# GEGLU on one core: eight first products ahead of the second ones, and another order of the first loads

## The chip, the cores and the metric

The kernel runs on one core of one Trainium2 chip. The metric is the device time of one execution in microseconds (us).

## The reference

```python
B, S, D, F = 32, 32, 1024, 3584        # x [32, 32, 1024], all bf16
def reference(x, w_gate, w_up, w_down):
    return (gelu_tanh(x @ w_gate) * (x @ w_up)) @ w_down
```

The 1024 rows of x are tokens. The output is [32, 32, 1024] in bf16.

## The kernel before

Both stages are block products of 2 x 2 halves done with seven multiplications instead of eight (sums and differences of the halves take the place of one product).

**Stage 1.** The left operand has w_gate and w_up as its two rows and the two halves of D as its columns: A11 and A12 are the low and the high half of D of w_gate, A21 and A22 those of w_up. The right operand is x transposed: B11 and B21 are the low and the high half of D for tokens 0 to 511, B12 and B22 the same for tokens 512 to 1023. F is cut into 28 blocks of 128 columns. For a block `i`:

- the first product A11 B11 and the second A12 B21 add up in one PSUM bank to w_gate's result for the first tokens. Each is four matmuls of 128x128 by 128x512 in bf16. Between them ScalarE copies the first product out to `E1` (an eviction), and after the second it applies GELU from the bank into `GL`;
- the five others (`fourth_product` to `seventh_products`, `third_product`) use sums in float32r: S1 to S4 of weights, T1 to T4 of x. A seed (`seed`) copies `E1` back into a bank, on which the sixth, seventh and fourth products go on.

First and second products run ahead of the rest by ten blocks (`LEAD`). The order of instructions on each engine is the order of the code (`tc.manual_schedule`), so each engine's queue is a list written by hand.

**Loads.** `load_gate(c, queue, lo, hi)` loads 256 columns of w_gate (blocks 2c and 2c + 1) and of them the slices lo to hi of the eight 128-row slices of D. Slices 0 to 3 (`0, KH`) are called the low half of gate c here, 4 to 7 (`KH, DT`) the high half; each is 256 KB. Gates 0 to 3 have buffers of their own, gates 4 and 5 lie in a part of `gT` that is written late. `load_up(c, lo, hi)` loads w_up. x comes by three transposing DMAs on SP's queue: B11 (L131), B21 (L147) and both halves for the later tokens, `xt1` (L154). DMAs are issued from two queues, SP (`nc.sync`) and ScalarE (`nc.scalar`). [...]

**Start.** While B11 is on its way TensorE runs ten warm-up matmuls on constants (L139) into four PSUM banks `warm`. After warm-up matmuls 3 and 7 ScalarE makes a small copy from the bank (L141), which delays the loads that stand behind it in ScalarE's queue.

**PSUM.** Eight banks in two rings of four: `psum_q` (tag "q") for first and second products and later `Y`, `psum_p` (tag "p") for the warm-up and then `X`.

**Order of TensorE before.** First products of blocks 0 and 1 (in two cuts of D), 2, 3; second products of 0 to 3; then for 4, 6 and 8 the first products of a pair, one operation on ScalarE (`between`), and its second products. After that come `Y` of blocks 0 and 1 with T1 (timeline: y<-T,s), first products of block 10, the sixth products with T2 (x<-T,s), and so on. VectorE makes S1 to S4 of blocks 0 and 1 from w_up's first load, then T1 to T4 (L165) when `xt1` has landed.

**Stage 2** is the same scheme with w_down and `gT`; the change does not touch it.

Of the kernel before, what the change touches and what calls it, by code (L numbers as in the profile page):

```python
# [7 lines left out]
ACT = mybir.ActivationFunctionType  # L8
# [4 lines left out]
def kernel(  # L13
# [18 lines left out]
    nc = tc.nc  # L32
# [10 lines left out]
    DT = D // P  # L43
    KH = DT // 2
# [31 lines left out]
    B11, B21 = xt0[:, :KH, :], xt0[:, KH:, :]  # L76
# [6 lines left out]
    def load_gate(c, queue, lo=0, hi=DT):  # L83
        if c not in WG:
            WG[c] = gw.tile([P, DT, 2 * P], bf16, name="gw", tag="gw")
        queue.dma_start(  # L86
            out=WG[c][:, lo:hi, :], in_=wg_r[:, lo:hi, 2 * c * P : (2 * c + 2) * P]
        )

    def load_up(c, lo=0, hi=4):  # L90
        if c not in WU:
            WU[c] = uw.tile([P, DT, 4 * P], bf16, name="uw", tag="uw")
        nc.sync.dma_start(
            out=WU[c][:, :, lo * P : hi * P],
            in_=wu_r[:, :, (4 * c + lo) * P : (4 * c + hi) * P],
        )
# [4 lines left out]
    def a11(i):  # L101
        return block(WG, 2, i, 0)

    def a12(i):
        return block(WG, 2, i, 1)
# [4 lines left out]
    def a22(i):  # L110
        return block(WU, 4, i, 1)
# [12 lines left out]
    def psum_p(name):  # L124
        return psum.tile([P, NB], fp32, name=name, tag="p")

    def psum_q(name):
        return psum.tile([P, NB], fp32, name=name, tag="q")

    with tc.manual_schedule():  # L130
# [4 lines left out]
        table = opool.tile([P, 8], bf16, name="table", tag="o")  # L135
        nc.scalar.activation(table, ones[:, 0:8], ACT.Gelu_apprx_tanh)  # L136

        for n in range(NWARM):
            nc.tensor.matmul(warm[n % 4], lhsT=ones[:, 0:P], rhs=ones, start=True, stop=True)  # L139
            if n in (3, 7):  # L140
                nc.scalar.activation(table, warm[n % 4][:, 0:8], ACT.Copy)  # L141
            if n == 3:
                load_gate(0, nc.scalar, 2, KH)
                load_gate(1, nc.scalar, 0, KH)
            if n == 7:
                load_gate(0, nc.scalar, KH, DT)
        nc.sync.dma_start_transpose(out=B21, in_=xf[0:NB, KH * P : D])  # L147
        load_gate(1, nc.sync, KH, DT)
        load_gate(2, nc.sync)
        load_gate(3, nc.sync, 0, KH)  # L150
        load_up(0, 0, 2)
        load_gate(3, nc.sync, KH, DT)
        load_gate(4, nc.sync)
# [8 lines left out]
        def t_sum(name, a, b, step=2):  # L162
            for k in range(0, KH, step):
                ks = slice(k, k + step)
                nc.vector.tensor_tensor(T[name][:, ks, :], a[:, ks, :], b[:, ks, :], ALU.subtract)  # L165
# [19 lines left out]
        def copy_a22(i):  # L185
            nc.scalar.activation(C22[i], a22(i), ACT.Copy)

        A, E1, GL = {}, {}, {}

        def pair_product(ps, lhs, rhs, first, cuts):  # L190
            for lo, hi in zip(cuts, cuts[1:]):
                for p, l in zip(ps, lhs):
                    for k in range(lo, hi):
                        nc.tensor.matmul(  # L194
                            p,
                            lhsT=l[:, k, :],
                            rhs=rhs[:, k, :],
                            start=(first and k == 0),
                            stop=(k == KH - 1),
                            skip_group_check=True,  # L200
                        )

        def first_products(*blocks, cuts=(0, KH)):
            for i in blocks:
                A[i] = psum_q("a")
            pair_product([A[i] for i in blocks], [a11(i) for i in blocks], B11, True, cuts)
            for i in blocks:
                if i % 2 == 0:
                    pool, tag = (xpool, "e1") if i == LEAD - 2 else (ring, "ring")
                    E1[i // 2] = pool.tile([P, 2, NB], fp32, name="e1", tag=tag)  # L210
                nc.scalar.activation(E1[i // 2][:, i % 2, :], A[i], ACT.Copy)  # L211

        def second_products(*blocks, cuts=(0, KH)):
            pair_product([A[i] for i in blocks], [a12(i) for i in blocks], B21, False, cuts)
            for i in blocks:
                if i % 2 == 0:
                    GL[i // 2] = half.tile([P, 2, NB], bf16, name="gl0", tag="half")
                nc.scalar.activation(GL[i // 2][:, i % 2, :], A[i], ACT.Gelu_apprx_tanh)
# [3 lines left out]
        def seed(i):  # L222
            X[i] = psum_p("x")
            nc.scalar.activation(X[i], E1[i // 2][:, i % 2, :], ACT.Copy)
# [3 lines left out]
        def ahead():  # L228
            nonlocal done
            if done < FT:  # L230
                first_products(done)
            second_products(done - 1)
            done += 1
# [40 lines left out]
        t_sum("T2", B22, T["T1"])  # L274
        t_sum("T3", B22, B12)
        t_sum("T4", B21, T["T2"])
        between = {4: lambda: seed(0), 6: lambda: seed(1), 8: lambda: copy_a22(0)}
        first_products(0, 1, cuts=(0, 2, KH))
        first_products(2)
        first_products(3)  # L280
        for n in range(4):
            second_products(n)
        for n in (4, 6, 8):
            first_products(n)
            first_products(n + 1)
            between[n]()
            second_products(n)
            second_products(n + 1)
        for k in range(KH):
            nc.scalar.activation(T["B22"][:, k, :], B22[:, k, :], ACT.Copy)  # L290
        copy_a22(1)
# [25 lines left out]
        for i in range(2, FT + 1):  # L317
# [24 lines left out]
            if here and i % 2 == 0:  # L342
                c = i // 2 + (6 if i < 8 else 4)
# [44 lines left out]
        B21 = lambda j: V21[j]  # L388
# [149 lines left out]
```

## Time and profile before

| | |
|---|---|
| time, median of 3 runs | 276.35 us (276.2 to 276.45) |
| profiled execution | 276.38 us, of which the span in the trace 274.6 us |
| TensorE clock granted | 1.00 over the whole span |
| last copy out of PSUM starts, last store issued | 271.25 us, 271.87 us |

Times in the views are counted from the start of the span. PE is TensorE, DVE VectorE, ACT ScalarE, POOL GpSimd, SP the engine that only issues; SPq and ACTq are the issues of DMAs on SP's and ScalarE's queue, and the length of such a row is how long the issue held the engine, not the transfer. In a timeline the columns are start, length, engine, line, operation, output <- inputs, shapes, number, and in brackets the idle time before the group and what ended it. In a row of a DMA queue stand packets, MB and the time that the packets took as a share of 16 engines. In a row of a DMA issue stand number, KB each and us from the start of the issue to the landing.

### The profile page before, as it was taken

To read this page: it belongs to the slowest core of one execution; us is meant where nothing else is said; L and a number is where in the kernel's file an instruction comes from. 1 tells how busy PE (TensorE), PEld (TensorE's weight loads), DVE (VectorE), ACT (ScalarE), POOL (GpSimd) and SP (SyncE) were. 2 spreads that over 40 slices of the span, in tenths; PEclk is the share of its full clock that TensorE was granted. 3 is DMA by queue.
4 is the path that set the end of the run, shared out by engine and by line. 5 is a ranking of instruction groups with operands and counts; after the bars stand their busy time and mean duration, and the time that the engine had idled before them with its cause. 6 is when DMAs were issued, how large, how long until landed. Compare 5 with 4: busy or idle time off the path is not lost.

```text
span 274.6 us, 3345 instructions
## 1 busy us (share of the span) xinstructions
PE 269.2 (98%) x1186; PEld 189.6 (69%) x1186; DVE 188.7 (69%) x226; ACT 138.1 (50%) x238; POOL 87.1 (32%) x81
## 2 busy tenths in 40 slices
PE   8899999999999999999999999999999999999995
PEld 2345667768777687776877768764447888888883
DVE  0078875866667666686666766769994999999900
ACT  2588665666556665566665666531100072860311
POOL 0000083845558455584455844600000000000000
PEclk9999999999999999999999999999999999999999
DMA  8999402153400034216260202359702000000321
GB/s 173 295 289 236 155 1 76 35 197 91 140 2 0 0 90 143 76 28 203 87 220 0 76 2 76 107 195 319 223 0 76 2 0 0 1 2 0 116 76 38
DMA packets 40992, 26.42 MB, mean 96 GB/s; under 512 B 9232, under 2 KB 40976, under 8 KB 40976
## 3 DMA queue, kind: packets, MB, share of 16 engines
q1 hardware_dynamic: 39232, 25.30, 31.9%
q10 hardware_dynamic: 1744, 0.92, 1.2%
q8 instruction: 9, 0.15, 0.2%
q14 instruction: 7, 0.06, 0.1%
HBM read 22.02 MB, written 2.10 MB: 88 GB/s over the span
## 4 chain that ended last, share of the span: by engine, by line
PE 96%; DMA 2%; ACT 1%; ACTq 0%; issue 0%
PE x L194 19%; PE x L393 18%; PE y L115 18%; PE a L194 17%; PE x L115 9%; PE y L393 9%; PE z L393 4%; DMA gw<-in_w_gate_dram 2%; PE y L194 1%; ACT L136 0%; ACTq L86 0%; ACT o_sb L505 0%; ACT table L136 0%; ACT table L141 0%
## 5 line engine op out<-in xcount | busy, mean ns | idle before, releaser
L194 PE MATMUL x<-T,s 128*128 128x512 f32 x224 | 63.5, 407 | 0.0
L194 PEld LDWEIGHTS x<-T,s 128*128 128x128 f32 x224 | 41.7, 188 | 10.7
L194 PE MATMUL a<-xt,gw 128*128 128x512 bf16 x192 | 44.8, 380 | 1.3 <-DMA gw<-in_w_gate_dram 0.8
L257 DVE TENSOR_TENSOR u<-y,e 128x512 bf16<-128x512 f32 x28 | 19.3, 691 | 33.2 <-ACT e L255 32.4
L183 POOL TENSOR_TENSOR s<-gw,s 128x512 fp32r<-128x512 bf16 x22 | 26.0, 1181 | 48.5 <-PE y L115 47.8
L194 PEld LDWEIGHTS <-gw 128*128 128x128 bf16 x192 | 17.3, 98 | 25.3 <-issue 5.7
L179 DVE TENSOR_TENSOR s<-s,gw 128x512 fp32r<-128x512 f32 x24 | 34.5, 1436 | 0.0
L264 ACT ACTIVATE gl<-h 128x512 bf16<-128x512 bf16 x28 | 17.7, 631 | 28.1 <-DVE h L262 28.1
L244 DVE TENSOR_TENSOR gT<-gl,x 128x512 bf16<-128x512 bf16 x28 | 19.2, 687 | 17.6 <-PE x L115 17.6
L115 PE MATMUL x<-T,c 128*128 128x512 f32 x112 | 30.3, 393 | 0.0
L115 PE MATMUL y<-B,s 128*128 128x512 f32 x112 | 30.2, 391 | 0.0
L174 POOL TENSOR_TENSOR s<-uw 128x512 fp32r<-128x512 bf16 x25 | 29.1, 1165 | 0.0
L115 PE MATMUL y<-T,s 128*128 128x512 f32 x104 | 27.8, 389 | 0.0
L211 ACT ACTIVATE e<-a 128x512 f32<-128x512 f32 x28 | 16.6, 597 | 18.7 <-PE a L194 18.6
L393 PE MATMUL x<-tc,sc 128*128 128x512 f32 x112 | 25.7, 389 | 0.0
L255 ACT ACTIVATE e<-x 128x512 f32<-128x512 f32 x28 | 16.7, 600 | 16.0 <-PE x L194 16.0
L175 POOL TENSOR_TENSOR s<-gw,uw 128x512 fp32r<-128x512 bf16 x21 | 24.4, 1162 | 0.0
L115 PEld LDWEIGHTS y<-B,s 128*128 128x128 f32 x112 | 21.0, 188 | 4.8
L115 PEld LDWEIGHTS x<-T,c 128*128 128x128 f32 x112 | 20.9, 188 | 4.8 <-ACT e L255 0.5
L393 PEld LDWEIGHTS x<-tc,sc 128*128 128x128 f32 x112 | 21.0, 188 | 4.4
L115 PEld LDWEIGHTS y<-T,s 128*128 128x128 f32 x104 | 19.5, 188 | 4.1
L393 PEld LDWEIGHTS <-gT 128*128 128x128 bf16 x112 | 10.9, 98 | 13.3 <-issue 0.3
(56 smaller groups left out, 347.0 us busy)
## 6 DMA issues: line engine op xcount, KB each, us to landing
uw<-in_w_up_dram SPq DMA_DIRECT2D x6, 1024.0 KB, 6.5
gw<-in_w_gate_dram SPq DMA_DIRECT2D x9, 512.0 KB, 4.0
v<-in_w_down_dram SPq DMA_DIRECT2D x5, 512.0 KB, 3.9
v<-in_w_down_dram SPq DMA_DIRECT2D x4, 640.0 KB, 8.2
v<-in_w_down_dram SPq DMA_DIRECT2D x8, 256.0 KB, 4.8
out_dram<-o_sb SPq DMA_DIRECT2D x15, 128.0 KB, 1.7
uw<-in_w_up_dram SPq DMA_DIRECT2D x2, 512.0 KB, 6.5
gT<-in_w_gate_dram SPq DMA_DIRECT2D x2, 512.0 KB, 5.8
```

The lines of the kernel that those rows point to most:

```text
L115: nc.tensor.matmul(ps, lhsT=lhs[:, k, :], rhs=rhs[:, k, :], start=(first and k == 0), stop=(k == KH - 1), skip_group_check=True,)
L174: engine.tensor_tensor(S1[i], a21(i), a22(i), ALU.add)
L175: engine.tensor_tensor(S3[i], a11(i), a21(i), ALU.subtract)
L179: nc.vector.tensor_tensor(S2[i], S1[i], a11(i), ALU.subtract)
L183: engine.tensor_tensor(S4[i], a12(i), S2[i], ALU.subtract)
L194: nc.tensor.matmul(p, lhsT=l[:, k, :], rhs=rhs[:, k, :], start=(first and k == 0), stop=(k == KH - 1), skip_group_check=True,)
L211: nc.scalar.activation(E1[i // 2][:, i % 2, :], A[i], ACT.Copy)
L244: nc.vector.tensor_tensor(gT[:, i, 0:NB], GL[i // 2][:, i % 2, :], X[i], ALU.mult)
L255: nc.scalar.activation(e3, X[i], ACT.Copy)
L257: nc.vector.tensor_tensor(U1[i], Y[i], e3, ALU.add)
L264: nc.scalar.activation(G1[i], h1, ACT.Gelu_apprx_tanh)
L393: nc.tensor.matmul(ps, lhsT=lhs[:, i, t * P : (t + 1) * P], rhs=rhs[:, i, :], start=(first and j == 0 and i == 0), stop=(last and j == JF ...
```

## The change

Of the loads: the low half of gate 2 goes to ScalarE's queue, behind those of gates 0 and 1. The high half of gate 0 moves from ScalarE's queue to SP's. On SP the low half of gate 3 comes right behind B21, then the high halves of gates 0, 1 and 2. ScalarE's second small copy follows warm-up matmul 8 instead of 7, and is followed by a new operation that writes 8 columns of B21; B21's transposing DMA writes the same place, so it must wait for that operation. All of SP's later DMAs stand behind it.

Of the products: the first products of blocks 0 to 7 all come ahead of the second products of blocks 0 to 7. Blocks 4 to 7 take their banks from the ring "p", so all eight banks are in use. The seeds of blocks 0 and 1 come between the GELUs of blocks 5, 6 and 7 on ScalarE. Blocks 8 and 9 follow as before. The number of matmuls, of DMAs' bytes and of all operations stays the same, but for the one new operation, and one DMA of 512 KB (gate 2) that becomes two.

```diff
         for n in range(NWARM):
             nc.tensor.matmul(warm[n % 4], lhsT=ones[:, 0:P], rhs=ones, start=True, stop=True)
-            if n in (3, 7):
+            if n in (3, 8):
                 nc.scalar.activation(table, warm[n % 4][:, 0:8], ACT.Copy)
             if n == 3:
                 load_gate(0, nc.scalar, 2, KH)
                 load_gate(1, nc.scalar, 0, KH)
-            if n == 7:
-                load_gate(0, nc.scalar, KH, DT)
+                load_gate(2, nc.scalar, 0, KH)
+            if n == 8:
+                nc.scalar.activation(B21[:, 0, 0:8], table, ACT.Copy)
         nc.sync.dma_start_transpose(out=B21, in_=xf[0:NB, KH * P : D])
-        load_gate(1, nc.sync, KH, DT)
-        load_gate(2, nc.sync)
         load_gate(3, nc.sync, 0, KH)
+        for c in range(3):
+            load_gate(c, nc.sync, KH, DT)
         load_up(0, 0, 2)
         load_gate(3, nc.sync, KH, DT)
         load_gate(4, nc.sync)
...
         def first_products(*blocks, cuts=(0, KH)):
             for i in blocks:
-                A[i] = psum_q("a")
+                A[i] = psum_p("a") if 4 <= i < 8 else psum_q("a")
...
-        between = {4: lambda: seed(0), 6: lambda: seed(1), 8: lambda: copy_a22(0)}
         first_products(0, 1, cuts=(0, 2, KH))
-        first_products(2)
-        first_products(3)
-        for n in range(4):
+        for n in range(2, 8):
+            first_products(n)
+        for n in range(8):
             second_products(n)
-        for n in (4, 6, 8):
-            first_products(n)
-            first_products(n + 1)
-            between[n]()
-            second_products(n)
-            second_products(n + 1)
+            if n in (5, 6):
+                seed(n - 5)
+        first_products(8)
+        first_products(9)
+        copy_a22(0)
+        second_products(8)
+        second_products(9)
```

## The prediction

> **What bounds the kernel now.** I read the page's first and fifth parts, then who waited for whom, then the stretches, and only then the first 30 us closely. Part 1 and one group of part 5:
>
> ```profile
> PE 269.2 (98%) x1186; PEld 189.6 (69%) x1186; DVE 188.7 (69%) x226; ACT 138.1 (50%) x238; POOL 87.1 (32%) x81
> ...
> L194 PE MATMUL a<-xt,gw 128*128 128x512 bf16 x192 | 44.8, 380 | 1.3 <-DMA gw<-in_w_gate_dram 0.8
> ```
>
> TensorE is busy for 98% of the span. The waits of TensorE and three stretches say where the rest is (columns of a stretch: its length, then busy us of each engine, granted clock, DMA share, GB/s):
>
> ```profile
> PE a L194 <- DMA gw<-in_w_gate_dram: 0.8, 1, 0.8
> PE a L194 <- DMA xt<-in_x_dram: 0.5, 1, 0.5
> ...
> 24.12:36.00 11.88, 11.88 (x53) 8.48 (x53) 10.90 (x14) 7.59 (x15) 1.18 (x2) 1.00 0.55 155
> 36.00:183.50 147.50, 147.50 (x653) 108.42 (x652) 97.40 (x131) 90.46 (x163) 85.72 (x76) 1.00 0.27 84
> 183.50:271.30 87.80, 87.71 (x393) 63.31 (x390) 72.56 (x71) 25.15 (x35) 0.00 (x0) 1.00 0.21 68
> ```
>
> From 24.12 us on TensorE never waits, at a granted clock of 1.00. The change keeps every matmul, so it can only win before that, and whatever it wins is carried to the end as long as nothing else becomes late. The TensorE timeline (start, length) and three pieces of the chain of waits:
>
> ```profile
> 0.77 4.43 PE L139 MATMUL warm<-const-bfloat16-1.0 128*128 128x512 bf16 x10 [0.77 <-PEq L522]
> 5.66 1.89 PE L194 MATMUL a<-xt,gw 128*128 128x512 bf16 x8 [0.46 <-DMA xt<-in_x_dram]
> 8.36 12.31 PE L194 MATMUL a<-xt,gw 128*128 128x512 bf16 x56 [0.81 <-DMA gw<-in_w_gate_dram]
> 23.77 2.19 PE L194 MATMUL y<-T,s 128*128 128x512 f32 x8
> 26.48 2.21 PE L194 MATMUL x<-T,s 128*128 128x512 f32 x8
> ...
> 3.16 5.15 DMA gw<-in_w_gate_dram
> ...
> 24.12 1.84 PE y L194 x8
> ...
> 37.78 1.74 PE a L194 x8
> ```
>
> Blocks 0 and 1 run at 5.66, when B11 has landed. Blocks 2 and 3 need the low half of gate 1, issued by ScalarE at 3.16 and landed 5.15 us later, at 8.31; TensorE goes on at 8.36. One bf16 matmul costs 1.74 / 8 = 0.2175 us, one f32r matmul 1.84 / 8 = 0.23 us.
>
> **Why that load is late.** The issues on SP and on ScalarE, with two small ScalarE operations (start, length):
>
> ```profile
> 0.74 1.42 SPq L131 DMA_TRANSPOSE xt<-in_x_dram  x1
> 2.21 3.67 SPq L147 DMA_TRANSPOSE xt<-in_x_dram  x1
> 5.93 2.11 SPq L86 DMA_DIRECT2D gw<-in_w_gate_dram  x3
> 19.30 0.58 SPq L86 DMA_DIRECT2D gT<-in_w_gate_dram  x1
> ...
> 2.48 0.21 ACT L136 ACTIVATE table<-const-bfloat16-1.0 128x8 bf16<-128x8 bf16 x1
> 2.76 0.90 ACTq L86 DMA_DIRECT2D gw<-in_w_gate_dram  x2
> 4.38 0.18 ACT L141 ACTIVATE table<-warm 128x8 bf16<-128x8 f32 x1 [1.46 <-PE warm L139]
> 13.80 0.60 ACT L218 ACTIVATE gl<-a 128x512 bf16<-128x512 f32 x1 [0.27 <-PE a L194]
> ```
>
> And the packets of the two queues (q1 is SP's, q10 is ScalarE's; packets, MB, share) in the windows 2.25 to 2.75, 2.75 to 3.45, 3.5 to 4.7, 4.8 to 5.3, 6.3 to 7.6 and 8.15 to 8.85 us:
>
> ```profile
> q1 hardware_dynamic: 311, 0.08, 69.8%
> ...
> q1 hardware_dynamic: 208, 0.05, 123.0%
> ...
> q1 hardware_dynamic: 1341, 0.34, 126.8%
> ...
> q10 hardware_dynamic: 248, 0.12, 93.0%
> ...
> q10 hardware_dynamic: 492, 0.25, 73.0%
> q1 hardware_dynamic: 518, 0.13, 50.0%
> ...
> q10 hardware_dynamic: 471, 0.24, 114.4%
> q1 hardware_dynamic: 1, 0.00, 0.2%
> ```
>
> From 3.5 to 4.7 q1 alone moves: B11 (2048 packets of 256 B). ScalarE's second gate load, issued at 2.76, flows only at 4.8, when B11 is nearly through. Then B21, issued at 2.21, takes its turn, and gate 1's low half (512 packets) shares with it packet by packet from 6.3 to 7.6: 492 against 518. So B21, which nobody needs before the second products, stands in front of a load that TensorE waits for.
>
> **The change part by part.**
>
> *B21 held.* The copy after warm-up matmul 8 comes one warm-up slot (4.43 / 10 = 0.44 us) after the copy of 4.38, so 4.82; it takes 0.18 and the write into B21 0.21, so SP's wait ends near 5.2 and B21 is issued at about 5.25 instead of 2.21. Queued behind it on SP are all other loads: gate 3 low, the three high halves, w_up, gate 4, xt1. On ScalarE the added operation costs 0.21 us before the first eviction, for which ScalarE waits anyway.
>
> *Gate lows first.* After B11 q10 holds 256 + 512 + 512 packets (gates 0, 1, 2). Alone, q10 moved 471 packets in 0.7 us, 673 a us, so they take 1.9 us: 4.8 to 6.7. Gate 1 low would be through at about 5.95 and gate 2 low at 6.7. Between last packet and use lay 8.31 - 7.6 = 0.7 us for gate 1 low, so they land at 6.65 and 7.4. TensorE needs them at 5.66 + 8 x 0.2175 = 7.40 and 5.66 + 16 x 0.2175 = 9.14. Both waits are gone.
>
> *What the wait is worth.* Before, matmul 24 ends at 8.36 + 16 x 0.2175 = 11.84. Without a wait it is 5.66 + 24 x 0.2175 = 10.88. The ceiling is 0.96 us, not the 0.81 of the waits row, which starts after the pipeline has drained.
>
> *What is late next: gate 3's low half*, wanted at 10.88, which is now behind B21 on SP. Further rows: q1 in the windows 18 to 20, 20.75 to 21.75 and 22 to 23, and the landings of the loads issued at 5.93 (gate 1 high) and 19.30 (gate 5):
>
> ```profile
> q1 hardware_dynamic: 2266, 0.58, 127.5%
> ...
> q1 hardware_dynamic: 153, 0.06, 26.3%
> ...
> q1 hardware_dynamic: 666, 0.34, 112.2%
> ...
> gw<-in_w_gate_dram SPq DMA_DIRECT2D x1, 256.0 KB, 4.7
> ...
> gT<-in_w_gate_dram SPq DMA_DIRECT2D x1, 512.0 KB, 4.8
> ```
>
> B11's first packets come 1.5 us after its issue (0.74 to 2.25), so B21's come at 6.75. A transpose alone runs at 2266 / 2 = 1133 packets a us: 2048 packets take 1.81 us, to 8.56. Behind a transpose q1 has a hole: after xt1 153 packets in a whole us. Gate 1 high landed at 5.93 + 4.7 = 10.63, 2.5 us after B21's last packet (about 8.15). Gate 5, of twice the size, landed at 24.1; less its second half (0.26 MB at 0.34 MB/us, 0.77 us) that is 23.3, 2.55 us after xt1's last packet (about 20.75). With 2.5 us gate 3 low lands at 8.56 + 2.5 = 11.06, and TensorE waits 0.18 us for it. The gain is 11.84 - 11.06 = 0.78 us. This wait has no row in the trace, so its bounds: nothing, if the hole is shorter by 0.2 us; 0.68 if a slow stretch like that of 2.75 to 3.45 (208 packets where 0.7 us at 1133 would carry 790, so 0.5 us lost) falls on this stream as well.
>
> *Second products later, and four more banks.* Second products now start after 32 matmuls, 11.06 + 8 x 0.2175 = 12.8 us. B21's packets are through 4 us before. Gate 0 high follows gate 3 low by 0.26 MB, 0.77 us: 11.8. An eviction takes 0.60 us (the row of 13.80) against 4 x 0.2175 = 0.87 us of matmuls for a block, with 0.27 us idle before it, so the banks that blocks 8 and 9 take are free long before. The two seeds, copies of the same size and so taken at 0.60 us each, delay a GELU or two by what eight such gaps give back; they are wanted only in the sixth products. Cost: nothing; without those gaps it would be their 1.2 us on ScalarE.
>
> *The sums of VectorE.* When gate 3 low lands, the stream has carried 2 MB (B11, B21, four halves); before, the same 2 MB had landed with gate 1 high at 10.63. So all that follows, xt1 with it, comes 0.43 us later, and TensorE is 0.78 us earlier:
>
> ```profile
> 21.33 2.50 DVE L165 TENSOR_TENSOR T<-xt,xt 128x512 fp32r<-128x512 bf16 x4 [1.00 <-DMA xt<-in_x_dram]
> 23.75 2.35 DVE L165 TENSOR_TENSOR T<-xt,T 128x1024 fp32r<-128x1024 bf16 x2
> ```
>
> T1 is whole at 23.83 and its last quarter wanted at 23.77 + 6 x 0.23 = 25.15: 1.32 us to spare. T2 is whole at 26.10, its second half wanted at 26.48 + 4 x 0.23 = 27.40: 1.30. The change uses 0.78 + 0.43 = 1.21. It just fits; if gate 3 low comes later, both terms move against each other and their sum stays.
>
> *Sum.* The profiled execution took 276.38 us (span 274.6, 1.78 around it); the median of the runs shown is 276.35, 0.03 below, so I carry the sum over unchanged: 276.38 - 0.96 + 0.18 = 275.6 us.
>
> **A rule against the change.** From 3.5 to 4.7 us q10 had an issued load and moved nothing, while from 6.3 to 7.6 both queues moved one packet for one. The Trainium skill ("DMA: Bandwidth & Descriptors", Queues, rings and completion order) says that each DMA engine goes round its queues packet by packet. By that rule the larger batch that ScalarE now queues would take turns with B11 itself. The first rival works this out from rows; the trace agrees with the rule in the second window and not in the first.
>
> **The rivals.**
>
> *B11 is slowed by the gate loads (slower).* It decides if what held ScalarE's load until 4.8 was B21 waiting in line, which is now gone. Then q10 starts about 1 us after its issue, at 3.8. By 1341 packets in 1.2 us some 1,100 of B11 are left then. Shared, they go at 518 / 1.3 = 398 a us and take 2.8 instead of 1.0 us; ScalarE's 1280 packets last long enough for that. B11 lands 1.8 us later, at 7.4, and matmul 24 ends at 12.6 instead of 11.84: 0.8 us slower, 277.2. If sharing starts only at 4.3, it is about equal to before. The break-even is a B11 landing at 6.6. Against it: the load of 2.76 flowed before B21 and not behind it, as it would if B21 had blocked it, and its issue stays at the same time. Chance 0.15.
>
> *The wait only moves.* Gate 3 low lands at 11.3 to 12.2 because B21 is issued as slowly as before (3.67 us), shares with the rest of q10, or a slow stretch falls in. The gain is 11.84 less that landing: 275.9 at 11.3, nothing at 11.84, 276.7 at 12.2. For it: the holes behind both other transposes. Against: nothing of B11 is left when B21 is issued. Chance 0.25.
>
> *VectorE's sums bind, or the hold does not help.* If xt1 comes 1 us later with no delay of gate 3, T2's slack of 1.30 leaves a gain of 0.3: 276.1. If gate 1 low was late for itself and not for B21, it lands at 8.3 again: 276.4. Chance 0.1 together.
>
> *B11 earlier.* The slow stretch from 2.75 us lies half a us behind B21's issue at 2.21. If B21 caused it, B11 lands up to 0.5 us earlier; gate 3 low is then the limit unless it comes earlier too. 275.2 to 275.4. Chance 0.05.
>
> **How the numbers follow.** Forecast 0.45, between 275.4 and 275.8. A measurement of this kernel can tell about 0.2% (0.55 us) from no change, so faster means below 275.8 and slower above 276.9. Faster: nearly all of the forecast and the last rival, a little of the moved wait: 0.50. Slower: most of the first rival, and the far end of the moved wait: 0.17. The same: 0.33. The range runs from the last rival's 275.2 to 277.0, which leaves out the slow end of the first rival.
>
> **What would show it.** Right: the waits of TensorE lose the 0.8 us on gw before matmul 9 and show one under 0.4 us before matmul 25; SP's second transpose is issued near 5.25; q10 flows without a break from 4.8 to 6.7. Wrong: matmul 1 starts later than 6 us (first rival), matmul 25 starts after 11.4 (moved wait), or TensorE waits between 24 and 28 us on DVE. Before, matmul 32 ends at 8.36 + 24 x 0.2175 = 13.58; the forecast is 12.8, and it falls if that matmul ends after 13.2.

## The result and the profile after

The changed kernel takes 276.06 us (median of 22 runs, 275.72 to 276.78); the kernel before, in alternation on the same chip, 276.73 us (22 runs, 276.09 to 279.29). The ratio is 0.997, with a 95% interval of 0.9957 to 0.9984. The lowest runs differ by 0.37 us, less than the medians, because the kernel before scatters upward. In the prediction's own terms 276.06 us lies in the band "the same" (275.8 to 276.9 us, given 0.33) and not in "faster" (below 275.8 us, given 0.50). The ratios here and below leave out each kernel's longest executions (over 1.5% above its fastest); the medians leave out none. The profiled execution took 276.09 us (span 274.3), 0.29 us less than that of before.

Part 1 of the page and TensorE's waits:

```profile
PE 268.9 (98%) x1172; PEld 189.3 (69%) x1186; DVE 188.6 (69%) x226; ACT 138.2 (50%) x239; POOL 87.2 (32%) x81
...
PE warm L139 <- PEq L523: 0.8, 1, 0.8
PE a L195 <- DMA xt<-in_x_dram: 0.5, 1, 0.5
```

The 0.8 us on gw is gone. The start on TensorE, ScalarE and SP (start, length, in brackets the idle time before), with the landing of gate 3's low half:

```profile
5.74 14.14 PE L195 MATMUL a<-xt,gw 128*128 128x512 bf16 x63 [0.54 <-DMA xt<-in_x_dram]
22.99 2.47 PE L195 MATMUL y<-T,s 128*128 128x512 f32 x8
25.98 2.21 PE L195 MATMUL x<-T,s 128*128 128x512 f32 x8
...
4.87 0.18 ACT L141 ACTIVATE table<-warm 128x8 bf16<-128x8 f32 x1 [1.95 <-PE warm L139]
5.08 0.21 ACT L147 ACTIVATE xt<-table 128x8 bf16<-128x8 bf16 x1
11.12 0.60 ACT L212 ACTIVATE e<-a 128x512 f32<-128x512 f32 x1 [0.27 <-PE a L195]
12.15 0.60 ACT L212 ACTIVATE e<-a 128x512 f32<-128x512 f32 x1 [0.44 <-PE a L195]
...
5.31 2.37 SPq L148 DMA_TRANSPOSE xt<-in_x_dram  x1
...
gw<-in_w_gate_dram SPq DMA_DIRECT2D x1, 256.0 KB, 3.3
```

All first and second products of blocks 0 to 7 are one group without a wait of its own. One short pause shows only on ScalarE: between the evictions of blocks 5 and 6 it idles 0.44 instead of 0.27 us, so TensorE waited about 0.17 us before matmul 25. That is gate 3's low half, issued at 7.74 and landed 3.3 us later, at 11.04. The `y` products start at 22.99 instead of 23.77: 0.78 us ahead, as forecast. But they take 2.47 instead of 2.19, and the `x` products start only 0.50 ahead. VectorE shows why. Its `u` and `h` are the first sums of finished products for the later tokens; the last row is ScalarE's GELU of `h`. First after, then before:

```profile
22.17 2.50 DVE L166 TENSOR_TENSOR T<-xt,xt 128x512 fp32r<-128x512 bf16 x4 [1.04 <-DMA xt<-in_x_dram]
24.59 2.35 DVE L166 TENSOR_TENSOR T<-xt,T 128x1024 fp32r<-128x1024 bf16 x2
...
31.40 1.28 DVE L258 TENSOR_TENSOR u<-y,e 128x512 bf16<-128x512 f32 x2
...
35.72 0.63 ACT L265 ACTIVATE gl<-h 128x512 bf16<-128x512 bf16 x1 [2.79 <-DVE h L263]
```

```profile
31.62 1.29 DVE L257 TENSOR_TENSOR u<-y,e 128x512 bf16<-128x512 f32 x2 [0.98 <-ACT e L255]
...
35.95 0.63 ACT L264 ACTIVATE gl<-h 128x512 bf16<-128x512 bf16 x1 [2.52 <-DVE h L262]
```

T1 starts 0.84 us later than before (22.17 against 21.33) and its last quarter is ready at 22.17 + 2.50 = 24.67, when the `y` products, 0.78 earlier, want it at 24.37. That gives back 0.27 us. Before, VectorE idled 0.98 us between T4 and `u`, waiting for ScalarE; now it has no idle time there and is itself late. ScalarE then waits 2.79 instead of 2.52 us for `h`: another 0.27 given back, which reaches TensorE through the evictions behind that GELU (between 37 and 43 us a weight load of TensorE waits for one of them, as none did before):

```profile
PEld x L195 <- ACT e L241: 0.3, 1, 0.3
```

In the timelines TensorE's lead over before runs:

| group on TensorE | before | after | lead |
|---|---|---|---|
| `y` of blocks 0 and 1 | 23.77 | 22.99 | 0.78 |
| first `x` | 26.48 | 25.98 | 0.50 |
| `y` at L115, second group | 34.90 | 34.40 | 0.50 |
| `y` with T at L115, second group | 42.17 | 41.93 | 0.24 |
| last copy out of PSUM (ScalarE) | 271.25 | 271.00 | 0.25 |

So a gain of 0.78 us was made by 23 us, and 0.25 of it was left by 42 us.

Why xt1 was 0.84 instead of the forecast 0.43 us late: its own packets first. SP's queue after, from 17.5 to 18.25 and from 18.5 to 20.5 us, and before, from 17.5 to 18.25 us, all inside xt1 (packets, MB, share):

```profile
q1 hardware_dynamic: 420, 0.11, 150.9%
...
q1 hardware_dynamic: 2266, 0.58, 127.5%
...
q1 hardware_dynamic: 852, 0.22, 127.8%
```

The second and the third are the normal rate, some 1133 packets a us. In the first, 0.75 us moved 420 instead of about 850; 430 are missing, 0.38 us. But this slow stretch does not explain the delay, which is there ahead of xt1 already. VectorE's first sum waits for w_up, which stands ahead of xt1 on SP's queue (before, then after):

```profile
15.17 0.69 DVE L174 TENSOR_TENSOR s<-uw 128x512 fp32r<-128x512 bf16 x1 [15.17 <-DMA uw<-in_w_up_dram]
...
15.97 0.69 DVE L175 TENSOR_TENSOR s<-uw 128x512 fp32r<-128x512 bf16 x1 [15.97 <-DMA uw<-in_w_up_dram]
```

It starts 0.80 us later. T1 follows it by 6.16 us before and 6.20 us after. In all eleven profiles here that load xt1 in one piece behind an undivided gate 4 the distance is 6.14 to 6.26 us, whether w_up lands early (14.88 us) or late (17.06). At gate 3's low half SP's stream was 0.41 us behind, as forecast (11.04 us, against 10.63 for gate 1's high half, which ended the same 2 MB before); at w_up it was 0.80. So the 0.4 us too many was lost between these two landings. What lost it is open: the packet rows add up all 16 engines and do not show whether some of them lagged.

### The profile page after: what moved, and what is told of

Read it like the earlier page. It is cut to its first block, busy times and chain, and to the rows that moved or that the text cites. A ratio compares the mean times of both kernels' runs of the same rounds, so it can differ in the third digit from the quotient of the medians.

```text
span 274.3 us, 3336 instructions
## 1 busy us (share of the span) xinstructions
PE 268.9 (98%) x1172; PEld 189.3 (69%) x1186; DVE 188.6 (69%) x226; ACT 138.2 (50%) x239; POOL 87.2 (32%) x81
## 4 chain that ended last, share of the span: by engine, by line
PE 96%; DMA 2%; issue 0%; ACT 0%
PE x L195 19%; PE x L394 18%; PE y L115 18%; PE a L195 18%; PE x L115 9%; PE y L394 9%; PE z L394 4%; DMA xt<-in_x_dram 2%; PE y L195 1%; ACT o_sb L506 0%
## 5 line engine op out<-in xcount | busy, mean ns | idle before, releaser
L195 PE MATMUL a<-xt,gw 128*128 128x512 bf16 x182 | 44.0, 380 | 1.1 <-DMA xt<-in_x_dram 0.5
L115 PE MATMUL x<-T,c 128*128 128x512 f32 x112 | 30.4, 393 | 0.0
L115 PE MATMUL y<-B,s 128*128 128x512 f32 x112 | 30.2, 391 | 0.0
L115 PE MATMUL y<-T,s 128*128 128x512 f32 x104 | 27.8, 389 | 0.0
L115 PEld LDWEIGHTS x<-T,c 128*128 128x128 f32 x112 | 20.9, 188 | 5.1 <-ACT e L256 0.7
L115 PEld LDWEIGHTS y<-B,s 128*128 128x128 f32 x112 | 21.0, 188 | 4.7
L115 PEld LDWEIGHTS y<-T,s 128*128 128x128 f32 x104 | 19.5, 188 | 4.1
```

The lines of the kernel that those rows point to most:

```text
L115: nc.tensor.matmul(ps, lhsT=lhs[:, k, :], rhs=rhs[:, k, :], start=(first and k == 0), stop=(k == KH - 1), skip_group_check=True,)
L195: nc.tensor.matmul(p, lhsT=l[:, k, :], rhs=rhs[:, k, :], start=(first and k == 0), stop=(k == KH - 1), skip_group_check=True,)
```

## The experiments

The theory: the changed loads bring the 0.78 us, and the late xt1, through T1 to T4, takes 0.5 of it away. Rivals: the hold does nothing and the order of the products is what counts; the wait for gates merely moves, to gate 3's low half; and, for each cure of the T chain, a new wait takes its place.

**The changed kernel again, on another chip.**

> The changed kernel itself, beside the three below. Its first profile shows TensorE 0.79 us ahead of before at the GELUs of blocks 8 and 9, 0.51 ahead from the sixth products on and 0.24 ahead from the evictions of block 2 on. If the second and third step come from xt1 (0.84 us later than before, of which some 0.4 us was a slow stretch in its own transfer), an execution with an earlier xt1 keeps more: with xt1 0.43 us late both steps are near nothing and the span is 0.5 us shorter (273.8). If the steps belong to the order of the products (ScalarE's queue, banks), they are the same in every execution, 0.24 us at the end.

276.31 us (276.1 to 276.94, 11 runs); before 277.11 (276.19 to 281.48, 29 runs); ratio 0.9963 [0.9934, 0.9992]. The lowest runs differ by only 0.09 us. This profile differs from the first (span 274.8):

```profile
5.11 5.49 PE L195 MATMUL a<-xt,gw 128*128 128x512 bf16 x24
12.12 8.81 PE L195 MATMUL a<-xt,gw 128*128 128x512 bf16 x40 [1.52 <-DMA gw<-in_w_gate_dram]
...
q1 hardware_dynamic: 291, 0.07, 100.6%
...
q1 hardware_dynamic: 44, 0.02, 43.4%
...
q1 hardware_dynamic: 225, 0.12, 80.3%
```

B11 comes 0.6 us earlier, which buys nothing: gate 3's low half comes a whole us later, and matmul 25 starts at 12.12, after the 11.84 of before. The rival in which the wait only moves holds in this execution. The three rows of SP's queue show where. From 7.25 to 7.75 us, inside B21, it moves 291 packets where the normal rate carries 567. But B21 also began earlier here, and by 9.3 us the queue is level again: 2028 packets since 6.4 us, against 2066 in the first profile since 6.8. Then comes the hole behind B21: from 9.5 to 10 us 44 packets here and 225 in the first profile (last row). So of the lost us this longer hole is the part that the rows show; what lengthens it is open.

**Without the hold.**

```diff
-            if n == 8:
-                nc.scalar.activation(B21[:, 0, 0:8], table, ACT.Copy)
```

> B21 is no longer held: the write into 8 columns of it is gone, all else is as changed. Theory (the gain is the wait for gate 1's low half, and the hold takes it away): B21 is issued at 2.2 us again and shares with gate 1's low half, which lands near 8.3; matmul 9 starts at 8.4, gate 2's and gate 3's low halves are there in time, xt1 lands at 21.3 as before: the time of before, ratio 1.000 (0.999 to 1.001). Rival (the order of the products or the gate loads ahead bring the gain, not the hold): as the changed kernel, 0.997.

276.45 us (276.06 to 281.0, 12); 0.9984 [0.9952, 1.0017]. In its profile:

```profile
5.36 2.14 PE L193 MATMUL a<-xt,gw 128*128 128x512 bf16 x8 [0.16 <-DMA xt<-in_x_dram]
8.27 12.26 PE L193 MATMUL a<-xt,gw 128*128 128x512 bf16 x56 [0.78 <-DMA gw<-in_w_gate_dram]
```

The 0.78 us wait for gate 1 is back, in the place it had before. So B21, issued early, is what makes that load late, as the prediction had it. The time alone would not have said so: its interval holds both no change and the changed kernel's ratio, and this profile's span, 274.3 us, is that of the changed kernel's first one. Its T1 starts at 21.29, so without the hold the T chain is not late. In these two profiles what the hold wins at the start and what it costs at the T chain are about even; but three of these 12 runs are over 277.5 us, and of the changed kernel's 33 none.

**T3 on GpSimd.** To shorten VectorE's chain.

```diff
-        def t_sum(name, a, b, step=2):
+        def t_sum(name, a, b, step=2, engine=nc.vector):
...
-                nc.vector.tensor_tensor(T[name][:, ks, :], a[:, ks, :], b[:, ks, :], ALU.subtract)
+                engine.tensor_tensor(T[name][:, ks, :], a[:, ks, :], b[:, ks, :], ALU.subtract)
...
-        t_sum("T3", B22, B12)
+        t_sum("T3", B22, B12, engine=nc.gpsimd)
```

> T3 is made on GpSimd, which is idle then, instead of VectorE; all else as changed. Theory (xt1 comes later, VectorE makes T1 to T4 in one piece and only then the sums of blocks 0 to 2, and that gives back the last 0.27 us): T4 ends 2.35 us earlier, VectorE waits for ScalarE's evictions again, TensorE stays 0.5 us ahead to the end: 0.25 us below the changed kernel. The wait for T1 at the first y products stays. T3 takes 4 x 1.17 = 4.7 us on GpSimd, from 22.2 to 26.9, and is wanted at 28.7. Rival (the loss sits in ScalarE's queue, where seeds and GELUs have moved): the same time as the changed kernel.

281.07 us (280.92 to 281.92, 4); 1.014 [1.0084, 1.0196]: slower, where 0.25 us less than the changed kernel was expected.

```profile
22.26 4.66 POOL L166 TENSOR_TENSOR T<-xt 128x1024 fp32r<-128x1024 bf16 x2 [21.82 <-DMA xt<-in_x_dram]
...
22.29 6.39 DVE L166 TENSOR_TENSOR T<-xt,xt 128x512 fp32r<-128x512 bf16 x4 [1.08 <-DMA xt<-in_x_dram]
...
PE y L195 <- DVE T L166: 2.9, 2, 1.8
```

While GpSimd makes T3, VectorE's T1 takes 6.39 instead of 2.50 us, and TensorE waits 2.9 us for it, in two pieces; from 29 to 31 us, behind them, its clock is at 0.50. The Trainium skill ("SBUF — State Buffer", Who interferes with whom) says that the two engines share a pair of SBUF ports under an exclusive lock. This trace agrees in that VectorE's sums take up to 2.65 us each while GpSimd's run, and 0.68 us once they are done; it does not show the ports. The run says nothing on the theory beyond this: T1 is on the path.

**Half of gate 4 behind xt1.** To bring xt1 forward.

```diff
-        load_gate(4, nc.sync)
+        load_gate(4, nc.sync, 0, KH)
         nc.sync.dma_start_transpose(out=xt1, in_=xf[NB:N, :])
+        load_gate(4, nc.sync, KH, DT)
```

> Gate 4 is loaded in two halves, the low one ahead of xt1 and the high one behind it; all else as changed. Theory (the loss is xt1's landing): 256 KB less stand ahead of xt1, 0.8 us; T1 starts near 21.4 instead of 22.2, the wait of the first y products for T1 goes and VectorE's sums are not late: TensorE keeps its 0.79 us, 0.5 us below the changed kernel (ratio to before 0.995). Gate 4's high half lands near 21.0 and is wanted at 21.4; if it is later by x, x is lost. Rival (order of the products): the same time as the changed kernel.

277.12 us (276.48 to 277.4, 12); 0.9988 [0.9956, 1.002].

```profile
11.86 8.81 PE L196 MATMUL a<-xt,gw 128*128 128x512 bf16 x40 [1.19 <-DMA gw<-in_w_gate_dram]
23.43 1.90 PE L196 MATMUL a<-xt,gT 128*128 128x512 bf16 x8 [1.04 <-DMA gT<-in_w_gate_dram]
24.98 2.20 PE L196 MATMUL y<-T,s 128*128 128x512 f32 x8
...
21.83 2.50 DVE L167 TENSOR_TENSOR T<-xt,xt 128x512 fp32r<-128x512 bf16 x4
```

T1 now starts directly behind VectorE's sums S1 to S4, without a wait for x, and the `y` products no longer wait for it. But the half of gate 4 behind xt1 comes through the hole that a transpose leaves on its queue: it was expected near 21.0, TensorE goes on at 23.43, and the wait costs 1.04 us. The cure of one wait made another, and the 0.5 us expected did not come.

**The order of products alone, and the loads alone.** The first keeps the loads of before with the changed products, the second the reverse; both diffs are against the changed kernel. The products alone:

```diff
-            if n in (3, 8):
+            if n in (3, 7):
...
-                load_gate(2, nc.scalar, 0, KH)
-            if n == 8:
-                nc.scalar.activation(B21[:, 0, 0:8], table, ACT.Copy)
+            if n == 7:
+                load_gate(0, nc.scalar, KH, DT)
         nc.sync.dma_start_transpose(out=B21, in_=xf[0:NB, KH * P : D])
+        load_gate(1, nc.sync, KH, DT)
+        load_gate(2, nc.sync)
         load_gate(3, nc.sync, 0, KH)
-        for c in range(3):
-            load_gate(c, nc.sync, KH, DT)
```

> The order of the products and the banks as changed, the loads as before. Theory (the gain is in the loads; eight first products in a row need them in the new order): gate 1's low half lands at 8.3 as before, gate 2 in one piece at 12.3 and is wanted at 10.1, so TensorE waits 2.2 us more and reaches the first y products at 26.2 instead of 23.8: 2.3 us slower than before. Rival (the order of the products brings the gain by itself): faster than before.

The loads alone:

```diff
-                A[i] = psum_p("a") if 4 <= i < 8 else psum_q("a")
+                A[i] = psum_q("a")
...
-        for n in range(2, 8):
-            first_products(n)
-        for n in range(8):
-            second_products(n)
...
+        first_products(2)
+        first_products(3)
+        for n in range(4):
+            second_products(n)
+        for n in (4, 6, 8):
...
```

> The loads as changed, the order of the products and the banks as before. Theory: the second product of block 0 is wanted at 9.1, but gate 0's high half is now behind B21 and gate 3's low half and lands near 11.9: a wait of 2.8 us takes the place of the one removed, 1.8 us slower than before. Rival (the loads alone bring the gain): faster than before by the 0.3% of the change.

280.42 us (280.15 to 281.01, 4), 1.0105 [1.0055, 1.0155], and 280.4 us (278.08 to 281.94, 10), 1.01 [1.0061, 1.0139]. Each half alone costs 1%; only together do they gain. Products alone, the timeline and two stretches, then both in one row (length, busy us of PE, PEld, DVE, ACT, POOL, granted clock, DMA share, GB/s):

```profile
8.56 1.90 PE L194 MATMUL a<-xt,gw 128*128 128x512 bf16 x8 [0.92 <-DMA gw<-in_w_gate_dram]
12.65 12.22 PE L194 MATMUL a<-xt,gw 128*128 128x512 bf16 x47 [2.18 <-DMA gw<-in_w_gate_dram]
27.97 1.28 PE L194 MATMUL y<-T,s 128*128 128x512 f32 x4
...
12.50:15.00 2.50, 2.35 (x7) 0.92 (x8) 0.00 (x0) 0.60 (x1) 0.00 (x0) 0.63 1.20 290
15.00:17.50 2.50, 2.50 (x9) 0.99 (x8) 2.14 (x4) 0.96 (x2) 0.00 (x0) 0.69 1.20 287
...
12.50:17.50 5.00, 4.85 (x15) 1.92 (x16) 2.14 (x4) 1.56 (x3) 0.00 (x0) 0.66 1.20 289
```

Loads alone:

```profile
12.74 13.49 PE L195 MATMUL a<-xt,gw 128*128 128x512 bf16 x47 [4.06 <-DMA gw<-in_w_gate_dram]
...
12.50:17.50 5.00, 4.76 (x12) 1.73 (x13) 1.12 (x2) 1.19 (x2) 0.00 (x0) 0.50 1.20 289
```

Waits were expected and the places are right: gates 2 and 3 behind B21 in the first, gate 0's high half behind everything in the second. The size was not. With products alone TensorE goes on with matmul 17 at 12.65; before, matmul 16 ends at 8.36 + 8 x 0.2175 = 10.10, so the waits put it 2.55 us behind. But the `y` products are 27.97 - 23.77 = 4.20 us behind. The other 1.65 us go with the granted clock, at 0.63 and 0.69 for five us after the wait: TensorE was busy for 4.85 of them with 15 matmuls, which take 15 x 0.2175 = 3.26 us at full speed. Loads alone shows the same, in the longest of its ten runs (281.94 us). Its wait was expected to end near 11.9 and ends at 12.74, 2.64 us behind before, but the `y` products start at 29.33, 5.56 us behind: the clock is at 0.50 for five us and at 0.75 for another 2.5. In both, the wait cost its length and then a slow stretch.

**ScalarE takes gate 3's low half.** The wait of matmul 25 is taken away without touching xt1.

```diff
                 load_gate(2, nc.scalar, 0, KH)
+                load_gate(3, nc.scalar, 0, KH)
             if n == 8:
                 nc.scalar.activation(B21[:, 0, 0:8], table, ACT.Copy)
+                load_gate(0, nc.scalar, KH, DT)
         nc.sync.dma_start_transpose(out=B21, in_=xf[0:NB, KH * P : D])
-        load_gate(3, nc.sync, 0, KH)
-        for c in range(3):
+        for c in range(1, 3):
```

> As changed, but gate 3's low half is a fourth load on ScalarE ahead of B21, and gate 0's high half is issued by ScalarE right behind the write into B21, so that it flows in the hole behind B21. Theory (what is left of the gain is lost to gate 3's low half behind B21, and to xt1 landing 0.8 to 1.4 us later through that hole): no wait before matmul 25 (seen: 0.17, 0.96, 1.19 and 1.52 us in four executions of loads in the changed order), gate 0's high half there before matmul 33, T1 starts at 21.3 to 21.8: 0.4 to 0.9 us below the changed kernel. Rival (the stream to xt1 is the limit and no order of it helps): the same time as the changed kernel.

276.5 us (276.06 to 276.89, 12); 0.9959 [0.9936, 0.9983].

```profile
12.70 7.07 PE L196 MATMUL a<-xt,gw 128*128 128x512 bf16 x31 [0.51 <-DMA xt<-in_x_dram]
23.63 2.54 PE L196 MATMUL y<-T,s 128*128 128x512 f32 x8 [0.41 <-DVE T L167]
...
22.88 2.50 DVE L167 TENSOR_TENSOR T<-xt,xt 128x512 fp32r<-128x512 bf16 x4 [1.10 <-DMA xt<-in_x_dram]
...
5.32 4.94 SPq L150 DMA_TRANSPOSE xt<-in_x_dram  x1
```

No wait for a gate is left, and the 0.4 to 0.9 us expected did not come. B21 now shares with ScalarE's loads (its issue holds SP for 4.94 us) and costs 0.51 us; T1 starts at 22.88, later still, and TensorE waits 0.41 us for it. With the gates cured, the x loads and the T chain set the time in this profile.

**The hold alone, in the kernel before.**

```diff
-            if n in (3, 7):
+            if n in (3, 7, 8):
...
+            if n == 8:
+                nc.scalar.activation(B21[:, 0, 0:8], table, ACT.Copy)
```

> The kernel before with B21 held by a warm-up as in the change and nothing else. Theory: gate 1's low half lands near 6.6 and its wait is gone, the second product of block 0 then waits for B21 (9.9 instead of 10.0): about 0.2 us faster than before at the low end of the runs. And the scatter: the kernel before has runs of 278 to 281 us (10 of 51), the one without the hold too (3 of 12), those with the hold none (49). If the hold takes these away, none of this kernel's runs is over 277.5; if they go away with the order of gate loads or products, they stay here.

276.77 us (276.26 to 279.21, 12, three of them over 279); 0.997 [0.993, 1.0011]. The profile is of one of the long executions (279.05 us):

```profile
11.07 12.21 PE L196 MATMUL a<-xt,gw 128*128 128x512 bf16 x47 [2.33 <-DMA xt<-in_x_dram]
...
12.50:15.00 2.50, 2.50 (x7) 0.88 (x6) 0.00 (x0) 0.83 (x2) 0.00 (x0) 0.50 1.13 306
```

In the old order second products come after 16 matmuls, and the held B21 is 2.33 us late for them (11.07, where 9.9 was expected); the clock then falls to 0.50. The nine shorter runs (276.26 to 277.31 us) were not profiled. The 0.2 us expected at the low end did not come: the lowest run is 276.26, before 276.28. The ratio is that of the changed kernel, so the times do not set the hold alone apart from the whole change. What they show is that the hold by itself does not take the long executions away; the expectation had left that open. The profiled long one lacks the other order, which puts 32 matmuls ahead of B21 instead of 16.

**xt1 in two transposes.** The first half of D lands earlier, and T1 reads only that.

```diff
-        nc.sync.dma_start_transpose(out=xt1, in_=xf[NB:N, :])
+        nc.sync.dma_start_transpose(out=B12, in_=xf[NB:N, 0 : KH * P])
+        nc.sync.dma_start_transpose(out=B22, in_=xf[NB:N, KH * P : D])
```

> As changed, but xt1 comes by two transposing DMAs, B12 ahead of B22, in the same place. Theory (what is given back after 22 us is VectorE's chain T1 to T4 behind the later xt1): T1 needs B12 alone, can start as soon as the sums of blocks 0 and 1 end (20.9 to 21.7) and is whole by 24.2; the wait of the first y products for T1 is gone, T4 ends 1 us earlier, and TensorE keeps what it has after the waits for gates: 0.25 to 0.5 us below the changed kernel where gate 3's low half is on time, about nothing where its wait is over 1 us. Rival (the loss after 22 us is ScalarE's queue or banks): the same time as the changed kernel.

275.7 us (275.4 to 275.97, 7); before on the same chip 276.44 (276.05 to 277.38, 14); 0.9968 [0.9957, 0.9979].

```profile
11.32 8.81 PE L196 MATMUL a<-xt,gw 128*128 128x512 bf16 x39 [0.92 <-DMA gw<-in_w_gate_dram]
23.23 2.20 PE L196 MATMUL y<-T,s 128*128 128x512 f32 x8
...
20.90 2.49 DVE L167 TENSOR_TENSOR T<-xt,xt 128x512 fp32r<-128x512 bf16 x4
31.09 1.29 DVE L259 TENSOR_TENSOR u<-y,e 128x512 bf16<-128x512 f32 x2 [0.90 <-ACT e L257]
...
35.42 0.63 ACT L266 ACTIVATE gl<-h 128x512 bf16<-128x512 bf16 x1 [2.52 <-DVE h L264]
```

T1 starts right behind the S sums, the `y` products take 2.20 us again, VectorE idles 0.90 before `u`, and ScalarE's wait for `h` is back at 2.52. Both give-backs are gone. In this execution gate 3's low half made TensorE go on at 11.32, which is worth 11.84 - 11.32 = 0.52 us; its lead over before is 0.54 us at the `y` products and 0.53 at the last copy out of PSUM (270.72 against 271.25). What is won at the start now reaches the end, as the theory has it. The times fit: on this chip, where the kernel before stays under 277.4 us, the lowest runs differ by 0.65 us, where the changed kernel's differed by 0.37 and 0.09.

**The same with the hold one warm-up earlier.**

```diff
-            if n in (3, 8):
+            if n in (3, 7):
...
-            if n == 8:
+            if n == 7:
```

> As the kernel before this one, and B21 held by warm-up matmul 7 instead of 8: issued near 4.9 instead of 5.3. Theory: B21, gate 3's low half and all behind it come 0.43 us earlier, gates 1 and 2 share a little more with B21 and are still in time; TensorE's wait before matmul 25 is 0.4 us shorter where there is one: 0.2 to 0.4 us below the kernel with xt1 in two. Rival (B21 then shares with ScalarE's loads and is no faster): no change.

275.77 us (275.49 to 275.94, 8); 0.9972 [0.9961, 0.9982]: no difference to the one before. B21 was issued at 4.83 here and at 4.76 there, because that execution's warm-up ran faster, so the profiles don't set the two apart.

These two have the lowest times. All 15 of their runs lie under 276 us, of the changed kernel's 33 ten. They did not run beside the changed kernel on one chip, and the ratios to the kernel before overlap, so the size of the advantage over it is open.

**The kernel before, profiled twice more,** for its scatter: it took over 277.5 us in 27 of 94 runs beside these experiments, the changed kernel in none of 33.

> The kernel before, to see where its scatter comes from (276.2 to 281.5 us in one set of 29 runs; the changed kernel 276.1 to 276.9). Theory: in some executions TensorE waits over 2 us before 13 us (gate or B21 late), and the granted clock then falls to 0.5 for 3 us or more, as seen at waits of 2.18, 2.33 and 4.06 us in other kernels (0.63 and 0.69, 0.50, 0.50 in stretches of 2.5 us) and not at 1.52, 1.19 or 1.04. If this execution is one of the long ones, its clock shows it between 8 and 18 us; if it is a short one (276.2 to 276.8), the clock is 1.00 throughout and no wait is over 1.5 us. Rival: a long execution has a clock of 1.00 and loses its time elsewhere.

> The kernel before once more, for the same question: a long execution (over 277.5 us) has a wait of TensorE over 2 us before 13 us and a clock of 0.5 behind it; a short one has neither. Rival: a long one at a clock of 1.00.

276.89 and 276.05 us, so neither is a long execution. They have waits of 0.97 and 1.25, and of 0.95 and 0.60 us at the start, and a clock of 1.00 in all stretches of the first 30 us. The second has a span of 274.3 us, that of the changed kernel's first profile: the 0.29 us between the first two profiles is within what one kernel does, and the account above rests on the waits and not on that difference. No long execution of the kernel before was profiled, so its waits stay open. Its runs give only a mean clock: on the two chips with most of them, 17 of the 18 runs over 278.6 us have 0.985 to 0.994, and the shorter ones 0.997 to 1.00; 0.006 of 276 us is 1.7 us, the size of the 1.65 found above. That long start-up waits bring the clock down there too fits this and is not shown.

## Why the prediction was right, and where it was not, step by step

- **Which wait, and why it was late: right.** The waits row on gw is gone, and comes back with 0.78 us when B21 is not held.
- **B21's hold: right, but the loads ahead of it were priced too low.** Copy at 4.87 (forecast 4.82), issue at 5.31 (5.25). ScalarE's queue flowed without a gap, but moved its 1273 packets from 4.8 to 7.2 us, 530 a us where the forecast took 673 and had them through at 6.7. Gates 1 and 2 still came in time.
- **Gate 3's low half: right in the first profile by luck, too small a term in general.** Forecast 11.06, landed 11.04. But B21's packets ran from about 7.2 to 9.2 us instead of 6.75 to 8.56, beginning when ScalarE's queue was through, and gate 3's low half landed some 1.9 us behind them instead of 2.5: two errors cancel. In the six profiles with these loads and this order of products (the changed kernel's two, T3 on GpSimd, half of gate 4, and both with xt1 split, one of them with the earlier hold), matmul 25 starts at 11.1, 11.32, 11.52, 11.61, 11.86 and 12.12. The upper bound of the prediction (0.68 us of wait, so 10.88 + 0.68 = 11.56) was passed three times, and its own sign that the wait had moved (matmul 25 after 11.4) shows in four. The rival "the wait only moves" was given 11.3 to 12.2 and a chance of 0.25; five of the six lie in it. It was the likelier case, and the forecast's 0.18 us was the term mis-sized.
- **VectorE's sums: the step that failed.** "It just fits", 1.21 of 1.30 us, has two faults. It carried the 0.43 us of gate 3's landing over to all that follows, where xt1 was 0.84 us late, 0.80 of it at w_up already: 0.78 + 0.84 = 1.62 against T1's slack of 1.32 makes 0.30 late; 0.27 was measured. The prediction had named such a wait for VectorE as a sign of being wrong. And it did not look at the row after that. VectorE's 0.98 us of idle time between T4 and `u` is a slack of the same kind, and the forecast's own 1.21 is more than it holds: some 0.2 us would have been given back even with xt1 as early as forecast. The rival "VectorE's sums bind" (276.1 us, a share of a chance of 0.1) comes nearest to what the first profile shows (276.09 us), though it looked for the wait at T2. The split xt1 confirms the chain: with T1 free again, both give-backs vanish.
- **B11 slowed by ScalarE's larger batch: did not happen.** Matmul 1 never started after 5.74. In seven of the nine profiles with the hold it started at 5.05 to 5.30, against 5.27 to 5.68 in the five without it: the last rival, B11 earlier, is true of most executions. It bought nothing, since gate 3 was then the limit, as that rival said.
- **Second products, banks, seeds: nothing, as forecast.** No wait is left in the group of matmuls after matmul 25, and no eviction is late.
- **The sum.** 275.6 forecast and 276.06 measured, within the range: -0.78 as forecast, +0.27 and +0.27 for the T chain, in the first profile. In the second the moved wait takes the place of these two, and TensorE is 0.29 us behind before at 42 us. That the ratio of 0.997 is also that of the forecast (275.6 / 276.38) is luck: the traces account for 0.25 of the 0.78 us, and the median is held against 276.73 us of a kernel whose long executions no trace explains.

What the expectations of two experiments missed altogether is what a long wait costs. Products alone and loads alone were expected to lose what they wait, and lost that and a slow clock on top. The Trainium skill ("TensorE: Matmul & The Clock Gate", Why this matters for your kernels) advises against idle gaps of TensorE above some 3 us, as they bring half speed back. Here a wait of 2.33 us was already followed by a clock of 0.50, and waits of 0.92 and 2.18 us two us apart by 0.63; a single one of 1.52 us was not. The measurement decides.

## What to carry to other kernels

When a change pulls one engine forward and pushes a load back, add both to the slack of every chain that the load feeds, link after link (here T1, then T4 and `u`). Price a load's delay by its own landing, not by that of an earlier one on the same queue, and with the spread between executions: here the same 256 KB landed between 11.04 and about 12.1 us. A product order and a load order belong together: each alone lost 1% here, and waits of 2.3 us and more cost more than their length when the clock gave way behind them. Issuing a transposing load as two, when one half is wanted first, freed T1 of its wait here (20.90 against 22.17).

## What the runs showed of the hardware

- TensorE's granted clock fell to 0.50 to 0.69 for 2.5 to 5 us after waits of 2.33 and 4.06 us near the start, after waits of 0.92 and 2.18 us two us apart, and after 1.12 and 1.80 us two us apart with T3 on GpSimd; after a single wait of up to 1.52 us it stayed at 1.00.
- The same loads behave differently from execution to execution. From 7.25 to 7.75 us, inside B21, SP's queue moved 425 packets in one execution of the changed kernel and 291 in another; in the hole behind B21, from 9.5 to 10 us, 225 and 44. Gate 3's low half landed behind it at 11.04 and at about 12.1 us.
- T1, which waits for xt1, started 6.14 to 6.26 us after VectorE's first sum, which waits for w_up's first load, in eleven profiles, wherever between 14.88 and 17.06 us that sum started.
- VectorE's four sums of T1 took 6.39 instead of 2.50 us beside two sums of GpSimd.
- The issue of B21's transpose held SP for 2.37 us in the changed kernel and for 4.94 us with two more gate loads of 256 KB on ScalarE's queue.
